# A transformer block on one core: gate/up with the activations held in TensorE, its product transposed by DMA

## The chip, the cores and the metric

The kernel runs on one core of one Trainium2 chip. The metric is the device time of one execution in microseconds; lower is better. Of the core's engines five appear below: TensorE (PE in the profile; PEld is its weight load), VectorE (DVE), ScalarE (ACT), GpSimd (POOL) and SyncE (SP), which here issues every DMA.

## The reference

One pre-norm block, sequence 2048, width 1024: attention with 32 query heads of 32 that share one key and value head, and a gated feed-forward of width 3584. All inputs and the output are bf16.

```python
def _A_ref(x, wq, wk, wv, wo):                 # H = 32, Dh = 32
    q = (x @ wq).reshape(B, S, H, Dh).transpose(0, 2, 1, 3)
    k = x @ wk
    v = x @ wv
    scores = jnp.einsum("bhqd,bkd->bhqk", q, k) * (Dh ** -0.5)
    p = _softmax(scores, axis=-1)
    o = jnp.einsum("bhqk,bkd->bhqd", p, v)
    return o.transpose(0, 2, 1, 3).reshape(B, S, H * Dh) @ wo
def _B_ref(x, w_gate, w_up, w_down):
    h = _sigmoid(x @ w_gate) * (x @ w_up)
    return h @ w_down
h  = x + _A_ref(_layernorm(x), A_wq, A_wk, A_wv, A_wo)
h2 = h + _B_ref(_layernorm(h), B_w_gate, B_w_up, B_w_down)
```

## The kernel before

**Tiles.** The sequence is cut into 16 query tiles of 128 tokens. Half a tile's heads (16) make a "half", so there are 32 halves; the two of one tile are a pair. For each half the loop runs over 16 key tiles. One such visit (`emit_S`, L650) is four matmuls of 512 columns, tiled four high in the array, into PSUM tile `S_ps`; two exponentials of 128x1024 on ScalarE (L668) write one of 12 buffers of `Pr` (a few other tiles serve as buffers at the start). `mk_PV` (L730) multiplies eight visits at a time with V, tiled four wide. Row sums of the softmax come in two ways: for halves in `RAW` (the first two) by matmuls with ones (the same `mk_PV`), for the others by adding the buffers on VectorE into `acc` (L643), then a selector matmul (`mk_SUM`, L694), a reciprocal, and a trip through DRAM that spreads the result (L707, L708). `mk_OP` (L818) is the output projection, to which the input is added; statistics and normalisation follow on VectorE and GpSimd (L337 to L356, L831), and a DMA transpose (L846) writes the normalised tile into `hnT`, with two tiles' room.

**Feed-forward.** The width 3584 is 7 groups of 512. `mk_GU` (L925) makes for each group a gate and an up group of matmuls: weights stationary (128x128), the tile's 128 tokens moving, so 32 matmuls of 128 columns into one PSUM bank of `F_ps`, whose output has the feed-forward channel on the partitions. ScalarE takes a tanh of the gate half (L961), VectorE multiplies (L967) and writes the product straight into `hact`, in the layout that the down projection reads. (A form with two tiles at once is in the code; the instructions of this kernel hold no matmul of that shape.) `mk_D` (L991) is the down projection: four groups of 28 matmuls of 256 columns, with `hact` stationary and the resident `w_down` (`wd_sb`) moving; VectorE adds the residual (L1004) and two DMAs store the tile (L1011).

**Weights.** Gate and up do not fit beside the rest and are loaded again for each tile, in slabs of 1 MB of four 256 KB loads each (`load_next`, L889, L908). Four slabs lie in `ring`; when the last visit has been issued, the buffers of `Pr` serve as slabs too. Tiles run the groups forth and back, so that two of seven are kept from one tile to the next.

**Order.** The program is written out by a planner (`Plan`) with costs of its own: each operation has an occupancy, a latency and a priority, and each engine's list is fixed when the program is built. A loop (L1044) gives TensorE one thing at a time: a visit when the planned backlog of ScalarE is under `run`, else the next matmul of the open group, else the next group of the queues `PV`, `SUM`, `OP`, `GU`, `D` and others. All groups but scores share the two banks of `F_ps`. Weight loads are paced in the plan (`pace`, bytes per ns), and the plan has a DMA rate (`rate`). SyncE's list is one queue in order: an issue that waits holds the ones behind it.

Of the kernel before, what the change touches and what calls it, by code (L numbers as in the profile page):

```python
# [12 lines left out]
P = 128  # L13
# [2 lines left out]
SEM = 75.0  # L16


TUNE = dict(swait=300, parts=2, raw=2, rl=0, nd=4, pc=16, rate=270, pace=280, xd=4, qf=2, dall=0, wo_late=1,
            nkn=3, few=0, rmin=700, hmin=1, h0=100, h1=350, hf=1.0, run=900, sum_few=0, pv_few=4, d_off=2,  # L20
            d_a=-1, d_b=0, eb=0, eq=700)


class Op:
# [16 lines left out]
class Plan:  # L41


    ENG = ("act", "dve", "pool", "sp")
    LATE = {"sl": 400.0, "rd": 300.0, "rb": 300.0, "hT": 400.0, "xt": 400.0}

    def __init__(self):
        self.lists = {e: [] for e in ("pe",) + self.ENG}
        self.free = {e: 0.0 for e in ("pe",) + self.ENG}
        self.heap = {e: [] for e in self.ENG}  # L50
        self.dma_free = 0.0
        self.pace_free = 0.0
        self.pe_mode = "dense"
        self.hold = (0.0, 0.0)
        self.seq = 0

    def op(self, eng, fn, deps=(), order=(), occ=60.0, lat=None, prio=5, key=None, nbytes=0, pace=False, tag=None):
# [23 lines left out]
    def need_end(self, d):  # L81
        while d.end is None:
            assert self.step(None), "plan is stuck"
        return d.end

    def start_of(self, o):

# [5 lines left out]
    def step(self, limit):  # L93
        best = None
        for e in self.ENG:
            h = self.heap[e]
            if h:
                s = min(self.start_of(o) for o in h)
                if best is None or s < best[0]:
                    best = (s, e)  # L100
        if best is None or (limit is not None and best[0] > limit):
            return False
        s, e = best
        h = self.heap[e]
        o = min((o for o in h if self.start_of(o) <= s + 1e-9), key=lambda o: (o.prio, o.seq))
        h.remove(o)
        if o.pace and self.pace_free > s:
            s2 = self.pace_free
            prev = [a for a in self.lists["act"][-6:] if a.end <= s2]
            if prev:  # L110
                o.deps.append(prev[-1])
            s = s2
        self.free[e] = s + o.occ
        o.start = s
        if o.nbytes:
            if o.pace:
                self.pace_free = s + o.nbytes / TUNE["pace"]
            go = max(s + 1500.0, self.dma_free)
            self.dma_free = go + o.nbytes / TUNE["rate"]
            o.end = self.dma_free + 750.0 + self.LATE.get(o.key.rstrip("0123456789"), 0.0)  # L120
        else:
            o.end = s + o.lat
        o.pos = len(self.lists[e])
        self.lists[e].append(o)
        for u in o.users:
            u.ready = max(u.ready, o.end)
            u.missing -= 1
            if u.missing == 0:
                self.heap[u.eng].append(u)
        o.users = []  # L130
        return True
# [21 lines left out]
def bass_sequential_preLN__grouped_kv_mqa__glu_gated_glu__prompt_kernel(  # L153
# [20 lines left out]
    NH = NT * 2  # L174
    NB = 3
    NHB = 3
    NSLAB = 4
    SW = 512
    NGR = NFT // 4
    NP = 12  # L180
    xf = A_x[0]
    of = out[0]

    with ExitStack() as es:
# [23 lines left out]
        hnT = SB("hnT", [DT, 2, P])  # L208
        hact = SB("hact", [NFT * 256])
        tnh = SB("tnh", [512], F32)  # L210
        st = SB("st", [8, 2, 6], F32)
        mv = SB("mv", [2, NT, 2], F32)
        mvb = SB("mvb", [2, NT, 2])
# [36 lines left out]
        pl = Plan()  # L250
        PE, ACT, DVE, POOL, SP = nc.tensor, nc.scalar, nc.vector, nc.gpsimd, nc.sync

        def dma(fn, key, nbytes, deps=(), prio=5, pace=False, order=()):
            return pl.op("sp", fn, deps, occ=450.0, key=key, nbytes=nbytes, prio=prio, pace=pace, order=order)

        def evac(fn_act, fn_dve, n, deps, prio, dve_rate=0.96, bias=0.0):
            now = pl.free["pe"]
# [126 lines left out]
        def x_by_dma(t):  # L384
# [2 lines left out]
                out=x_sb(t), in0=x_sb(t), scalar1=rstd[:, 0, t:t + 1], scalar2=None, op0=ALU.mult),  # L387
                [xcent[t], sv1[t][1]], prio=1, occ=330, lat=500)
            xT_ev[t] = dma(lambda: SP.dma_start_transpose(xnT[:, t // 4, :, (t % 4) * P:(t % 4 + 1) * P], x_sb(t)),
                           f"xt{t}", P * D * 2, [xnorm[t]], prio=0)  # L390
            ring_free(t)
            queue_after_xT(t)
            if t == NT - 1:
# [448 lines left out]
        def load_hT(t):  # L842

            if t not in hnorm or t in hT_ev or (t >= 2 and (t - 2) not in gu_last):
                return
            hT_ev[t] = hT_last[t] = dma(lambda: SP.dma_start_transpose(hnT[:, :, t % 2, :], hn[:, :]), f"hT{t % 2}", P * D * 2,  # L846
                                        [hnorm[t], gu_last.get(t - 2)] + (extra_rel if t < 2 else []), prio=0)


        ffn_next = [0]  # L850
# [3 lines left out]
        def start_ffn():  # L854
            t = ffn_next[0]
            if queues["GU"] or t >= NT or t not in hT_ev or (t and (t - 1) not in gu_last):
                return
            if t + 1 in hT_ev:
                ts = (t, t + 1)
            elif t + 1 in hnorm and hnorm[t + 1].end is not None:  # L860
                return
            else:
                ts = (t,)
            p = n_pass[0]
            n_pass[0] += 1
            ffn_next[0] += len(ts)
            load_next([])
            d_due.clear()
            nd = len(queues["D"])
            for i in range(NGR):  # L870
                for k in range(len(ts)):
                    mk_GU(p, ts, i, k)
            for k in range(nd):

                d_due.append(len(queues["GU"]) * (nd - k + TUNE["d_a"]) // (nd + 1 + TUNE["d_b"]))
# [3 lines left out]
        def group_of(p, i):  # L879
            return i if p % 2 == 0 else NGR - 1 - i  # L880
# [35 lines left out]
        hact_ev = {}  # L916
        box = {}

        def gu_deps(ts):
            return [d for t in ts for d in ([d_last[t - 2]] if t >= 2 else q_store[-NQS:] if t else extra_rel)]  # L920

        def gu_gate(p, ts, i, w):
            return (p, i, w) in slab_at and all((t == 0 or q_left[0] == 0) if t < 2 else d_done[t - 2] == ND for t in ts)

        def mk_GU(p, ts, i, k):  # L925

            gr = group_of(p, i)
            n = P * len(ts)
            fs = range(4) if len(ts) == 1 else range(2 * k, 2 * k + 2)
            f0 = 4 * gr + fs[0]  # L930
            hs = hact[:, :].rearrange("p (a f b) -> p a f b", a=2, b=P)[:, :, f0:f0 + len(fs), :]
            if len(ts) == 1:
                ho = hs[:, ts[0] % 2, :, :].rearrange("p f b -> p (f b)")
                mv_h = hnT[:, :, ts[0] % 2, :]
            else:
                ho = hs.rearrange("p a f b -> p a (f b)")
                mv_h = hnT[:, :, :, :]

            def shape(ap):
                return ap if len(ts) == 1 else ap.rearrange("p (a n) -> p a n", a=2)  # L940

            def bank_of(b, x):
                if len(ts) == 1:
                    return F_ps[:, b, x * P:(x + 1) * P]
                return F_ps[:, b, :].rearrange("p (a f b) -> p f a b", a=2, f=2)[:, x]

            def atoms(w):
                def a(b):
                    us, ops = slab_at[(p, i, w)]
                    return [(mm(bank_of(b, x), us[dt // 4][:, dt % 4, f * P:(f + 1) * P], mv_h[:, dt, :],  # L950
                                dt == 0, dt == DT - 1), n, "dense",
                             [ops[dt // 2]] if x == 0 and dt % 2 == 0 else [])
                            for x, f in enumerate(fs) for dt in range(DT)]
                return a

            def free(w, last):
                if i < NGR - 2 and fs[-1] == 3:
                    load_next([(u, [last]) for u in slab_at[(p, i, w)][0]])

            def after_g(b, last):  # L960
                box["a"] = pl.op("act", lambda: ACT.activation(out=tnh[:, :], in_=F_ps[:, b, :], func=ACTF.Tanh, scale=0.5),  # L961
# [2 lines left out]
                return [box["a"]]  # L964

            def after_u(b, last):
                e = pl.op("dve", lambda: DVE.scalar_tensor_tensor(  # L967
                    out=ho, in0=shape(tnh[:, :]), scalar=1.0, in1=shape(F_ps[:, b, :]),
                    op0=ALU.add, op1=ALU.mult), [last, box["a"]] + gu_deps(ts), prio=0, **t_dve(512))
                box["e"] = e  # L970
                for t in ts:
                    for f in fs:
                        hact_ev[(t, 4 * gr + f)] = e
                free(1, last)
                if i == NGR - 1 and fs[-1] == 3:
                    for t in ts:
                        gu_last[t] = last
                        load_hT(t + 2)
                        for dq in range(ND):
                            queues["D"].append(mk_D(p, t, dq))  # L980
                return [e]

            queues["GU"].append(Group("GU", atoms(0), lambda: [hT_ev[t] for t in ts] + slab_at[(p, i, 0)][1][0:TUNE["nkn"]], after_g,
                                      lambda: gu_gate(p, ts, i, 0)))
            queues["GU"].append(Group("GU", atoms(1), lambda: slab_at[(p, i, 1)][1][0:TUNE["nkn"]], after_u,
                                      lambda: gu_gate(p, ts, i, 1)))

        ND = TUNE["nd"]
        DW = D // ND
# [44 lines left out]
        def all_done(v):  # L1034

            v_done[0] = v
            if v == NV:
                all_S[0] = True
                load_next([(s.rearrange("p (d f) -> p d f", d=4), rel) for s, rel in free_slots])

        def known(deps, t):
# [208 lines left out]
```

## Time and profile before

| | |
|---|---|
| three runs | 1120.37, 1120.96, 1124.36 us (median 1120.96) |
| profiled execution | 1120.97 us, span 1118.9 us, TensorE clock 1.00 |
| TensorE busy | 1087.6 us (97%), 14987 instructions |
| TensorE weight load | 737.2 us (66%) |
| VectorE busy | 825.4 us (74%) |
| ScalarE busy | 1005.9 us (90%) |
| GpSimd busy | 57.8 us (5%) |
| DMA | 221.28 MB, mean 198 GB/s |

The span runs from the first to the last instruction; what lies around it is 2.07 us. A row of the page's groups reads: line, engine, operation, output<-input with shapes, count, then busy time and mean ns of one, then idle time ahead of it and what ended most of it. A matmul's mean is its passage through a pipeline, much longer than the spacing at which matmuls follow each other; spacing is read from the timeline, whose rows give a start, a length and a count. In a row of the busy time by stage, each engine has its busy us and number of instructions, then come the granted clock, the DMA engines' mean busy share and GB/s.

### The profile page before, as it was taken

What the parts mean: (1) busy time and instruction counts of PE and PEld (TensorE: products, weight loads), DVE (VectorE), ACT (ScalarE), POOL (GpSimd) and SP (SyncE); (2) the same over time, 40 slices, a digit from 0 to 9 for tenths busy, and PEclk for the clock granted to TensorE, in tenths of its full rate; (3) what the DMA queues carried; (4) which work ended last, traced back from release to release, by engine and by line L of the source; (5) the groups of instructions that cost most, each with busy time, mean ns of one, the idle gap of its engine ahead of it and who ended that gap; (6) DMA issues with size and microseconds to landing.
All of it is one profiled execution on the core that took longest, in us unless ns stands there. A gap on an engine that the chain in (4) does not pass through costs nothing.

```text
span 1118.9 us, 34515 instructions
## 1 busy us (share of the span) xinstructions
PE 1087.6 (97%) x14987; PEld 737.2 (66%) x15016; DVE 825.4 (74%) x1034; ACT 1005.9 (90%) x1155; POOL 57.8 (5%) x97
## 2 busy tenths in 40 slices
PE   6999998999999999999999999999999999999999
PEld 5533555756676766757666666766666766767898
DVE  8727888588878878688888778778788767877211
ACT  4898999999999999999999999999999999994010
POOL 5100100000000101010100001000001001000000
PEclk9999999999999999999999999999999999999999
DMA  9883695845848593846847495665747576479990
GB/s 257 184 272 114 149 309 180 258 144 181 265 122 253 161 282 88 254 136 206 234 124 218 128 282 140 212 207 163 209 140 218 154 219 201 142 219 288 289 291 16
DMA packets 244343, 221.28 MB, mean 198 GB/s; under 512 B 47456, under 2 KB 230752, under 8 KB 244192
## 3 DMA queue, kind: packets, MB, share of 16 engines
q1 hardware_dynamic: 244192, 219.07, 66.3%
q8 instruction: 119, 1.95, 0.7%
q14 instruction: 32, 0.26, 0.1%
HBM read 203.55 MB, written 8.11 MB: 189 GB/s over the span
## 4 chain that ended last, share of the span: by engine, by line
ACT 63%; PE 25%; DVE 5%; issue 5%; DMA 2%; SPq 1%; DVEq 0%
ACT Pr L668 59%; PE F_ps L416 22%; ACT tnh L961 4%; PE S_ps L416 3%; DMA rb<-r_scratch 1%; DVE acc L643 1%; DVE st L339 1%; DVE st L337 1%; SPq L708 0%; DVE ring L374 0%; DVE ring L386 0%; DMA ring<-in_B_w_gate_dram 0%; DMA ring<-in_A_x_dram 0%; PE F_ps L435 0%; DVE oun L759 0%
## 5 line engine op out<-in xcount | busy, mean ns | idle before, releaser
L668 ACT ACTIVATE Pr<-S_ps 128x1024 bf16<-128x1024 f32 x1008 | 957.7, 1193 | 6.3 <-PE S_ps L416 5.9
L643 DVE TENSOR_TENSOR acc<-acc,Pr 128x2048 bf16<-128x2048 bf16 x420 | 513.3, 1222 | 53.6 <-ACT Pr L668 39.6
L416 PE MATMUL F_ps<-hnT,ring 128*128 128x128 bf16 x6784 | 434.2, 219 | 2.1 <-issue 1.4
L416 PEld LDWEIGHTS F_ps<-hnT,ring 128*128 128x128 bf16 x6784 | 383.9, 98 | 67.0 <-issue 61.0
L416 PE MATMUL F_ps<-zone,hact 128*128 128x256 bf16 x1792 | 227.4, 273 | 0.1
L416 PE MATMUL S_ps<-QTb,kT 32*128 32x512 bf16 x2048 | 202.0, 385 | 7.1 <-ACT Pr L668 5.4
L416 PEld LDWEIGHTS F_ps<-zone,hact 128*128 128x128 bf16 x1792 | 162.8, 98 | 47.3 <-issue 27.8
L961 ACT ACTIVATE tnh<-F_ps 128x512 f32<-128x512 f32 x112 | 85.9, 767 | 75.2 <-PE F_ps L416 75.2
L967 DVE SCALAR_TENSOR_TENSOR hact<-tnh,F_ps 128x512 bf16<-128x512 f32 x112 | 76.5, 683 | 84.5 <-PE F_ps L416 83.4
L416 PE MATMUL F_ps<-Pr,Vt 128*32 128x512 bf16 x2016 | 133.4, 382 | 1.8 <-DVE h_sb L1004 1.0
L416 PEld LDWEIGHTS S_ps<-QTb,kT 32*128 32x128 bf16 x2048 | 51.5, 91 | 123.3 <-ACT Pr L668 86.7
L416 PEld LDWEIGHTS F_ps<-Pr,Vt 128*32 128x32 bf16 x2016 | 44.4, 96 | 57.0 <-issue 19.2
L416 PE MATMUL F_ps<-zone 128*128 128x512 bf16 (+3 forms) x572 | 73.7, 273 | 3.4 <-DVE mv L341 1.0
L416 PE MATMUL F_ps<-wo_sb,OT 128*128 128x512 bf16 x239 | 60.4, 380 | 3.8 <-DVE oun L759 1.4
L416 PEld LDWEIGHTS F_ps<-zone 128*128 128x128 bf16 x584 | 39.0, 98 | 30.3 <-issue 9.7
L350 POOL TENSOR_SCALAR zb<-mvb 128x1 bf16<-128x1 bf16 (+1 forms) x25 | 5.8, 233 | 986.8 <-DVE mvb L346 986.6
L1004 DVE SCALAR_TENSOR_TENSOR h_sb<-F_ps,h_sb 128x256 bf16<-128x256 f32 x64 | 26.9, 420 | 38.4 <-PE F_ps L416 38.2
L705 DVE RECIPROCAL r_sb<-F_ps 128x64 f32<-128x64 f32 x30 | 16.7, 558 | 36.2 <-PE F_ps L416 35.7
L416 PEld LDWEIGHTS F_ps<-wo_sb,OT 128*128 128x128 bf16 x256 | 21.6, 97 | 30.3 <-issue 8.1
L763 DVE TENSOR_TENSOR oun<-F_ps,oun 128x512 f32<-128x512 f32 x32 | 21.9, 686 | 21.8 <-PE F_ps L416 21.7
L643 DVE TENSOR_TENSOR acc<-Pr 128x2048 bf16<-128x2048 bf16 x30 | 35.0, 1165 | 0.0
L266 DVE CAST hact<-F_ps 128x512 bf16<-128x512 f32 (+1 forms) x25 | 16.3, 653 | 17.1 <-PE F_ps L416 15.2
(73 smaller groups left out, 329.9 us busy)
## 6 DMA issues: line engine op xcount, KB each, us to landing
ring<-in_B_w_gate_dram SPq DMA_DIRECT2D x304, 256.0 KB, 4.3
ring<-in_B_w_up_dram SPq DMA_DIRECT2D x304, 256.0 KB, 4.3
rb<-r_scratch SPq DMA_DIRECT2D x120, 64.0 KB, 2.7
zone<-in_B_w_down_dram SPq DMA_DIRECT2D x14, 512.0 KB, 4.8
Pr<-in_B_w_gate_dram SPq DMA_DIRECT2D x24, 256.0 KB, 4.6
Pr<-in_B_w_up_dram SPq DMA_DIRECT2D x24, 256.0 KB, 4.8
ring<-in_A_x_dram SPq DMA_DIRECT2D x16, 256.0 KB, 6.1
h_sb<-in_A_x_dram SPq DMA_DIRECT2D x16, 256.0 KB, 2.7
```

The costliest lines, as they stand in the source:

```text
L266: lambda: DVE.tensor_copy(out=out_ap, in_=in_ap))
L337: a = pl.op("dve", lambda s=s, src=src: DVE.bn_stats(st[:, s, 0, :], src[:, 0:512]), dp, prio=prio, occ=600, lat=756, order=[st_user.get(s)])
L339: b = pl.op("dve", lambda s=s, src=src: DVE.bn_stats(st[:, s, 1, :], src[:, 512:1024]), dp, prio=prio, occ=600, lat=756, order=[st_user.ge ...
L350: f = pl.op("pool", lambda: POOL.tensor_scalar(out=zb[:, ph, tk], in0=mvb[:, ph, tk, 1], scalar1=LN_EPS_BF16, scalar2=None, op0=ALU.add), ...
L416: return lambda: PE.matmul(o, lhsT=l, rhs=r, start=start, stop=stop, **kw)
L643: add_op[(hf, kt)] = pl.op("dve", lambda: DVE.tensor_tensor(out=a, in0=in0, in1=slot, op=ALU.add), dp, prio=6, **t_dve(2048, 1.92))
L668: exps[u] = pl.op("act", lambda i=i, pb=pb: ACT.activation(out=slot[:, i * 1024:(i + 1) * 1024].rearrange("p (a b) -> p a b", a=2), in_=S_ ...
L705: rc = pl.op("dve", lambda: DVE.reciprocal(r_sb[:, :], F_ps[:, b, 0:64]), [last, rd_ld.get(hf - 1)], prio=0, occ=64 * 8 / 0.96 + 20, lat=6 ...
L763: oun_ev[(hf, part)] = pl.op("dve", lambda: DVE.tensor_tensor(out=o, in0=F_ps[:, b, :], in1=o, op=ALU.add), [last, oun_ev[(hf, part - 1)]] ...
L961: box["a"] = pl.op("act", lambda: ACT.activation(out=tnh[:, :], in_=F_ps[:, b, :], func=ACTF.Tanh, scale=0.5), [last, box.get("e")], prio= ...
L967: e = pl.op("dve", lambda: DVE.scalar_tensor_tensor(out=ho, in0=shape(tnh[:, :]), scalar=1.0, in1=shape(F_ps[:, b, :]), op0=ALU.add, op1=A ...
L1004: e = pl.op("dve", lambda: DVE.scalar_tensor_tensor(out=h_sb[:, t % NHB, sl], in0=F_ps[:, b, 0:DW], scalar=0.5, in1=h_sb[:, t % NHB, sl], ...
```

## The change

Gate and up turn their operands around. The tile's normalised, transposed tokens (128x128 blocks of `hnT`) are stationary, and 512 columns of a weight slab move: 8 matmuls of 512 columns for a group in place of 32 of 128. The output then has tokens on the partitions. The product goes to one of three small buffers `act_s`, and a DMA transpose of 128x512 on SyncE's queue writes it into `hact` in the old layout; what waited for the product (the down projection) waits for that DMA. The form with two tiles is gone.

Beside this: the buffers of `Pr` are 11 instead of 12; `RAW` holds the first half only (`raw=1`), so the second half's sums go by VectorE adds and a selector matmul; transposes have a longer occupancy in the plan; near both ends (before 200 us of the plan, and after the last visit) the plan has another pace and rate than between; and several planner settings differ. The planner then writes all lists anew.

```diff
-TUNE = dict(swait=300, parts=2, raw=2, rl=0, nd=4, pc=16, rate=270, pace=280, xd=4, qf=2, dall=0, wo_late=1,
-            nkn=3, few=0, rmin=700, hmin=1, h0=100, h1=350, hf=1.0, run=900, sum_few=0, pv_few=4, d_off=2,
-            d_a=-1, d_b=0, eb=0, eq=700)
+TUNE = dict(pace0=280, rate0=300, swait=100, parts=2, raw=1, rl=0, nd=4, pc=16, rate=300, pace=250, xd=4, qf=2,
+            dall=1, wo_late=1, nkn=1, few=0, rmin=600, hmin=3, h0=200, h1=350, hf=1.0, run=700, sum_few=0,
+            pv_few=3, d_off=0, d_a=1, d_b=1, eb=0, eq=100)
...
+    def fast(self, s):
+
+        return s < 200000.0 or s > self.t_last
...
-                self.pace_free = s + o.nbytes / TUNE["pace"]
+                self.pace_free = s + o.nbytes / TUNE["pace0" if self.fast(s) else "pace"]
             go = max(s + 1500.0, self.dma_free)
-            self.dma_free = go + o.nbytes / TUNE["rate"]
+            self.dma_free = go + o.nbytes / TUNE["rate0" if self.fast(s) else "rate"]
...
+    NST = 3
...
-    NP = 12
+    NP = 11
...
+        act_s = SB("act_s", [NST, 512])
...
-                    us, ops = slab_at[(p, i, w)]
-                    return [(mm(bank_of(b, x), us[dt // 4][:, dt % 4, f * P:(f + 1) * P], mv_h[:, dt, :],
-                                dt == 0, dt == DT - 1), n, "dense",
-                             [ops[dt // 2]] if x == 0 and dt % 2 == 0 else [])
-                            for x, f in enumerate(fs) for dt in range(DT)]
+                    us, ops = slab_at[(t, i, w)]
+                    return [(mm(F_ps[:, b, :], hnT[:, dt, t % 2, :], us[dt // 4][:, dt % 4, :], dt == 0, dt == DT - 1),
+                             512, "dense", [ops[dt // 2]] if dt % 2 == 0 else []) for dt in range(DT)]
...
             def after_u(b, last):
+                k = n_act[0]
+                n_act[0] += 1
+                so = act_s[:, k % NST, :]
                 e = pl.op("dve", lambda: DVE.scalar_tensor_tensor(
-                    out=ho, in0=shape(tnh[:, :]), scalar=1.0, in1=shape(F_ps[:, b, :]),
-                    op0=ALU.add, op1=ALU.mult), [last, box["a"]] + gu_deps(ts), prio=0, **t_dve(512))
+                    out=so, in0=tnh[:, :], scalar=1.0, in1=F_ps[:, b, :],
+                    op0=ALU.add, op1=ALU.mult), [last, box["a"], act_dma.get(k - NST)], prio=0, **t_dve(512))
                 box["e"] = e
-                for t in ts:
-                    for f in fs:
-                        hact_ev[(t, 4 * gr + f)] = e
+                act_dma[k] = dma(lambda: SP.dma_start_transpose(ho, so), f"ha{t % 2}_{gr}", P * 1024, [e] + gu_deps(t),
+                                 prio=0, occ=700.0)
+                for f in range(4):
+                    hact_ev[(t, 4 * gr + f)] = act_dma[k]
...
             if v == NV:
                 all_S[0] = True
+                pl.t_last = pl.free["pe"]
```

## The prediction

> **What bounds the kernel now.** I read the page's slices and busy table first, then the chain that ended last, then the busy time by stage, then the timeline of TensorE.
>
> The slices (tenths busy, 40 slices of 28 us) and the groups that carry the work:
>
> ```profile
> PE   6999998999999999999999999999999999999999
> ACT  4898999999999999999999999999999999994010
> ACT 63%; PE 25%; DVE 5%; issue 5%; DMA 2%; SPq 1%; DVEq 0%
> L668 ACT ACTIVATE Pr<-S_ps 128x1024 bf16<-128x1024 f32 x1008 | 957.7, 1193 | 6.3 <-PE S_ps L416 5.9
> L416 PE MATMUL F_ps<-hnT,ring 128*128 128x128 bf16 x6784 | 434.2, 219 | 2.1 <-issue 1.4
> L416 PE MATMUL F_ps<-zone,hact 128*128 128x256 bf16 x1792 | 227.4, 273 | 0.1
> ```
>
> ScalarE is full until slice 36 (the exponentials), then nearly idle; TensorE is full to the end. The chain gives ScalarE 63% and TensorE 25%, the latter mostly at the end. So there are two stages: one in which exponentials and matmuls are both near their limit, and a tail that is TensorE alone. The stages, cut where score groups 1, 33, 97 and 481 start and where the last, the 512th, ends; the fourth row is a stretch of the tail:
>
> ```profile
> core 0: us, PE busy (x) PEld busy (x) DVE busy (x) ACT busy (x) POOL busy (x), PEclk, DMA share, GB/s
> 16.60:86.70 70.10, 66.94 (x718) 34.91 (x724) 40.56 (x104) 62.98 (x74) 11.41 (x18) 1.00 0.86 223
> 210.30:955.70 745.40, 737.36 (x10440) 498.49 (x10451) 587.63 (x675) 744.14 (x849) 29.97 (x36) 1.00 0.64 191
> 1016.50:1119.00 102.50, 98.72 (x1398) 90.78 (x1395) 31.23 (x49) 11.11 (x18) 1.34 (x3) 1.00 0.71 216
> 1020.00:1090.00 70.00, 69.05 (x1047) 63.60 (x1048) 23.15 (x36) 7.76 (x13) 1.34 (x3) 1.00 0.96 293
> ```
>
> Busy time cannot choose between the two engines in the middle: both are over 98%. The start-to-start spacing in TensorE's timeline can:
>
> ```profile
> 703.30 1.85 PE L416 MATMUL F_ps<-hnT,ring 128*128 128x128 bf16 x30
> 705.08 0.40 PE L416 MATMUL S_ps<-QTb,kT 32*128 32x512 bf16 x4
> 1097.15 3.22 PE L416 MATMUL F_ps<-zone,hact 128*128 128x256 bf16 x28
> 1100.21 3.74 PE L416 MATMUL F_ps<-hnT,ring 128*128 128x128 bf16 x64
> 1103.78 12.39 PE L416 MATMUL F_ps<-zone,hact 128*128 128x256 bf16 x112
> ```
>
> 64 gate/up matmuls from 1100.21 to 1103.78: 55.8 ns each. 28 down matmuls from 1097.15 to 1100.21: 109.3 ns each. 30 gate/up matmuls before a score group take 1.78 us, 0.11 more than 30 x 55.8 ns: that is what a change of tile position mode costs. In the same way a 512-column matmul (output projection) is 215.7 ns and a group of four tiled 512-column ones (scores, PV) 0.216. With these prices the counted work from 273 to 955 us fills all but 11.5 us. In the middle TensorE is packed, and ScalarE (64 exponentials x 0.905 plus 6.5 tanh x 0.48 = 61.0 us of a 62.1 us stretch per query tile) is just behind it.
>
> **The change, part by part.** I counted both programs' instruction orders with those prices, stage by stage. "Pair" is the two halves of a query tile (32 score groups).
>
> Gate/up: 7168 matmuls x 55.8 ns = 400.0 us become 1792 x 215.7 ns = 386.5: -13.5 us of TensorE. Weight loads fall to a quarter, but lay beside the matmuls already (PEld 67% of the middle), so nothing more for them. Row sums of the second half by ones-matmuls go to DVE adds and one selector sum: -64 tiled matmuls (16 groups x 0.216 = -3.5), +0.4. Total TensorE work counted: 1079.0 before, 1061.5 after.
>
> Where it goes (us; "counted" is TensorE's counted work):
>
> | stage | measured | counted | counted after | forecast |
> |---|---|---|---|---|
> | to first score | 16.6 | 4.4 | 5.6 | 17.8 |
> | pair 1 | 70.1 | 65.9 | 62.1 | 66.3 |
> | pair 2 | 62.3 | 60.7 | 60.1 | 61.7 |
> | pair 3 | 61.3 | 56.5 | 52.6 | 61.2 |
> | pairs 4-15 | 745.4 | 733.2 | 743.6 | 752.6 |
> | pair 16 | 60.8 | 59.9 | 60.3 | 61.2 |
> | last score to last matmul | 99.7 | 98.4 | 77.1 | 83.0 |
> | last store | 2.7 | - | - | 2.7 |
> | sum | 1118.9 | | | 1106.5 |
>
> To the first score: 7 more 256-column and 8 more 128-column matmuls stand ahead of it, +1.2. Pairs 1, 2 and 16 keep their stalls (4.2, 1.6, 0.9). Pair 3 is ScalarE's: 64 x 0.905 + 6 x 0.48 = 60.8 plus 0.4, so TensorE's saving of 4 there is lost. Pairs 4-15: the new order runs exactly one query tile of gate/up (112 matmuls) and down (112) in each pair, 61.95 us counted against 61.1; the stalls of 1.0 a pair shrink to 0.75, since those ahead of score and PV groups (3.3 of the 11.5 us) were waits on exponentials, and ScalarE (57.9 + 7 x 0.48 = 61.3) now has room. So the middle gets longer by 7 us: saved TensorE time is spent there on more feed-forward work. The tail gets it back: after the last score 960 gate/up matmuls (53.6) become 184 (39.7), 355 down (38.8) become 288 (31.5): -21.2.
>
> A second sum by ScalarE agrees: 4 more tanh (1.9) and 4 more evacuations (1.3) before the last exponential, first score 1.2 later: last score at 1016.5 + 4.4 = 1020.9; the table gives 1020.8.
>
> The tail's forecast is 77.1 + 1.4 (its old stalls) + 1.5 + 3. The 1.5 is new latency: the last product (0.68 us on DVE) now passes through a crossbar transpose before the down projection's last four matmuls of the first quarter can read it. Transposes of 256 KB land 3.1 to 5.7 us after issue, 128 KB stores in 2.4; I take 3.2 for 128 KB. Cover is 24 down matmuls, 2.6 us: 0.68 + 3.2 - 2.6 = 1.3, with a semaphore 1.5 (bounds 0.5 to 3.8). For earlier tiles and groups the transpose hides behind the next group (1.7 us) and behind down work that starts later.
>
> The 3 is DMA. The trace of before has 28 transposes, and one stands alone in a quiet stretch:
>
> ```profile
> 310.00:312.00 2.00, 2.00 (x35) 1.67 (x34) 0.54 (x2) 2.00 (x4) 0.00 (x0) 1.00 0.11 21
> 312.00:314.00 2.00, 2.00 (x36) 1.67 (x34) 0.00 (x0) 2.00 (x4) 0.00 (x0) 1.00 0.59 110
> ```
>
> 256 KB at share 0.59 + 0.11 over 2 us: 1.4 us of all engines; weight loads at 293 GB/s and share 0.96 cost 0.86 for 256 KB. So 0.7 us for each of the 112 new 128 KB transposes; a fit of share on bytes over all 2 us windows gives about 1.0 under load. The Trainium skill speaks otherwise (Advanced Engine Details and Errata, X-Bar Transpose (TRN2)): transposes run as fast as regular DMAs, 350-400 GB/s, an estimated 0.35 us each. By the page the new transposes take 39 us of DMA time in all, by the trace 78 to 112. In the middle neither matters: 7 transposes a pair add 5 to 7 us to DMA engines that are busy for 40 of 62 (share 0.64), and no wait for weights shows on TensorE. In the tail it does. After the last row sum 56 loads (48 us), 11 transposes, one of 256 KB (1.4) and five small rows (2): 56 us by the page, 59 to 63 by the trace. TensorE's work there is 72 us, of which the last 14 need no load, so 58 us. Before, 60 loads had 71 us by the same count and finished at about 1092, 10 us ahead of their last use. I take 3 us of stall (0 to 8).
>
> Costed at nothing: SyncE gets 112 issues x 0.65 us (half of the 1.3 us of a 256 KB one): 4.6 us of a 62 us pair in which loads take some 24. DVE gains 15 adds (1.2 us each) in pair 1, where it is 58% busy. One exponential buffer less: if that is not free it delays pair 1, where 2 us either way lie in the range. Other pacing of loads moves issues; TensorE showed no wait for them.
>
> Span 1106.5; the profiled execution took 1120.97 for a span of 1118.9, so 1108.6. That execution stands at the median (1120.96).
>
> **Rivals.** *Tail starved by DMA, or stalls in the middle that grow*: transposes cost 1.0 us or more under load, prefetch is thin (18 slabs left to use after the last sum, 14 of them still to load; before, 21 and 15), stall 8 instead of 3; or 1.2 us of stalls a pair instead of 0.75 (+5). For it: share 0.96 in the old tail. Against: the order holds down chunks between gate/up groups. 1113 to 1118.
>
> *Middle cheaper than counted*: stalls nearly vanish (0.3 a pair, -5), pair 1 falls to ScalarE's 62 (-4), tail without DMA stall (-3). 1097 to 1102.
>
> *Slower: SyncE's one queue.* Each transpose waits there for its DVE product, and the weight loads behind it wait too. In a dense gate/up stretch (699.8 to 709.2: 122 matmuls, 3.8 slabs) a slab is used up each 2.5 us, so the four-slab ring turns in 10; reissue takes 2.4 to 3.5 us and 4.3 to land, a margin of 2 to 3. Two transposes a round take 1.3 of it; if products come over half a microsecond later than their place, it is gone. It decides when the mean stall on TensorE passes 12.4 / 112 = 0.11 us a transpose; 0.2 gives 22 us, 1131. For it: order on SP is fixed. Against: SP sits waiting for buffer releases over 300 us in the waits, so it has time; no weight wait before.
>
> **How the numbers follow.** Forecast as summed (1103 to 1112): 0.58. Starved tail or middle stalls: 0.20. Cheaper: 0.13. SyncE queue: 0.09. 0.5% of 1121 is 5.6 us, about what a measurement here can tell from none. Faster by more (below 1115.4): 0.58 + 0.13 + two thirds of 0.20 = 0.84. Same: the rest of the 0.20 and a third of the 0.09, 0.10. Slower 0.06. The range leaves out a tenth on each side: 1100 to 1118.
>
> **What would show it.** Right: gate/up spacing 216 ns; last score at 1021 +-4; pairs 4-15 at 62.5 to 63; tail 80 to 86; a gap of 1 to 2 us on TensorE ahead of the last down matmuls. Wrong: TensorE waiting on weight DMA in the middle; score pairs above 64 us; a transpose landing after 5 us; tail over 90.

## The result, and the profile after

The changed kernel takes 1111.09 us (median of four runs, 1109.93 to 1111.60) against 1120.76 before: ratio 0.9905, 95% interval 0.9883 to 0.9927. The same kernel run again later (e5 below, called the control) gave 0.9901 (0.9887 to 0.9916). The forecast was 1108.6, range 1100 to 1118. The profiled execution took 1111.35 us with a span of 1109.6.

The page of the changed kernel, slices, chain and the three groups that answer to those shown before:

```profile
PE   5899987999999999999999999999999999999998
ACT  4899999999999999999999999999999999999110
PE 80%; ACT 9%; DVE 4%; DMA 4%; issue 2%; SPq 1%; POOL 0%; DVEq 0%; ACTq 0%
L675 ACT ACTIVATE Pr<-S_ps 128x1024 bf16<-128x1024 f32 x1008 | 945.6, 1061 | 9.3 <-PE S_ps L423 9.1
L423 PE MATMUL F_ps<-ring,hnT 128*128 128x512 bf16 x1672 | 413.6, 381 | 3.7 <-DMA ring<-in_B_w_gate_dram 2.5
L423 PE MATMUL F_ps<-zone,hact 128*128 128x256 bf16 x1792 | 231.0, 275 | 1.0 <-DMA hact<-act_s 0.6
```

The end of ScalarE's full stretch has moved one slice closer to the end of the span: the tail of TensorE alone is shorter. The chain has turned over, from ScalarE 63% and TensorE 25% to TensorE 80% and ScalarE 9%, although both engines are as busy as before. And new releasers stand behind the matmuls: weight DMAs (2.5 us) and the transposes (0.6 us).

Two pieces of TensorE's timeline (start, length, what, count):

```profile
309.14 2.12 PE L423 MATMUL F_ps<-ring,hnT 128*128 128x512 bf16 x9
311.19 0.40 PE L423 MATMUL S_ps<-QTb,kT 32*128 32x512 bf16 x4
...
1091.58 0.61 PE L423 MATMUL F_ps<-Pr,hnT 128*128 128x512 bf16 x2 [0.29 <-DMA Pr<-in_B_w_up_dram]
1092.47 1.32 PE L423 MATMUL F_ps<-Pr,hnT 128*128 128x512 bf16 x4 [0.29 <-DMA Pr<-in_B_w_up_dram]
1093.63 2.78 PE L423 MATMUL F_ps<-zone,hact 128*128 128x256 bf16 x24
1096.99 9.78 PE L423 MATMUL F_ps<-zone,hact 128*128 128x256 bf16 x88 [0.58 <-DMA hact<-act_s]
```

Nine gate/up matmuls and a mode change take 2.05 us: 9 x 215.7 ns + 0.11, the counted price. At the end two waits for weights (0.29 us each) and, after 24 down matmuls of the last tile, the wait for the last transpose: 0.58 us.

Busy time by stage: the third pair, pairs 4 to 15, and the last score to the end (busy us and instructions by engine, then clock, DMA share, GB/s):

```profile
150.20:215.90 65.70, 56.95 (x497) 21.82 (x496) 49.27 (x56) 62.25 (x71) 2.40 (x3) 0.95 0.91 236
215.90:964.50 748.60, 748.22 (x6722) 330.03 (x6721) 595.27 (x684) 747.86 (x853) 36.38 (x36) 1.00 0.80 211
1025.50:1109.60 84.10, 78.31 (x556) 48.14 (x552) 20.76 (x36) 8.73 (x14) 1.34 (x3) 1.00 0.90 240
```

The stages in us, where scores start and end as read from the timeline (the ends of the start and of the middle are exact to some tenths):

| | before | forecast | after |
|---|---|---|---|
| start: to the end of pair 3 | 210.3 | 207.0 | 215.9 |
| of it first score, pairs 1, 2, 3 | 16.6, 70.1, 62.3, 61.3 | 17.8, 66.3, 61.7, 61.2 | 19.5, 68.3, 62.4, 65.7 |
| middle: pairs 4 to 16 | 806.2 | 813.8 | 809.6 |
| tail: to the end of the span | 102.4 | 85.7 | 84.1 |
| span | 1118.9 | 1106.5 | 1109.6 |

The tail gives 18.3 us, the middle takes 3.4 back, the start 5.6. (The window of pairs 4 to 15 above ends 0.2 us short: pair 16 starts at 964.7.) Two questions follow: is the gain the cheaper matmuls, and what lengthens the start?

### The profile page after: what moved, and what is told of

It is laid out like the page before. It is cut to its first block, busy times and chain, and to the rows that moved or that the text cites. A ratio compares the mean times of both kernels' runs of the same rounds, so it can differ in the third digit from the quotient of the medians.

```text
span 1109.6 us, 23778 instructions
## 1 busy us (share of the span) xinstructions
PE 1076.8 (97%) x9608; PEld 488.4 (44%) x9608; DVE 836.5 (75%) x1039; ACT 1009.6 (91%) x1160; POOL 65.7 (6%) x97
## 4 chain that ended last, share of the span: by engine, by line
PE 80%; ACT 9%; DVE 4%; DMA 4%; issue 2%; SPq 1%; POOL 0%; DVEq 0%; ACTq 0%
PE F_ps L423 67%; PE S_ps L423 13%; ACT Pr L675 8%; DMA ring<-in_B_w_gate_dram 1%; DVE acc L650 1%; DMA rb<-r_scratch 1%; DVE st L344 1%; DVE st L346 1%; ACT tnh L944 1%; DMA Pr<-in_B_w_up_dram 0%; SPq L715 0%; DMA r_scratch<-r_sb 0%; SPq L907 0%; DMA ring<-in_A_x_dram 0%; DVE ring L381 0%
## 5 line engine op out<-in xcount | busy, mean ns | idle before, releaser
L675 ACT ACTIVATE Pr<-S_ps 128x1024 bf16<-128x1024 f32 x1008 | 945.6, 1061 | 9.3 <-PE S_ps L423 9.1
L650 DVE TENSOR_TENSOR acc<-acc,Pr 128x2048 bf16<-128x2048 bf16 x430 | 525.3, 1222 | 80.8 <-ACT Pr L675 65.8
L423 PE MATMUL F_ps<-ring,hnT 128*128 128x512 bf16 x1672 | 413.6, 381 | 3.7 <-DMA ring<-in_B_w_gate_dram 2.5
L423 PE MATMUL F_ps<-zone,hact 128*128 128x256 bf16 x1792 | 231.0, 275 | 1.0 <-DMA hact<-act_s 0.6
L423 PEld LDWEIGHTS F_ps<-ring,hnT 128*128 128x128 bf16 x1672 | 142.7, 98 | 192.6 <-issue 60.2
L423 PEld LDWEIGHTS F_ps<-zone,hact 128*128 128x128 bf16 x1792 | 163.9, 98 | 68.3 <-issue 34.2
L944 ACT ACTIVATE tnh<-F_ps 128x512 f32<-128x512 f32 x112 | 70.7, 631 | 57.3 <-PE F_ps L423 57.3
L953 DVE SCALAR_TENSOR_TENSOR act_s<-tnh,F_ps 128x512 bf16<-128x512 f32 x112 | 76.7, 684 | 39.5 <-PE F_ps L423 37.7
L423 PE MATMUL F_ps<-zone 128*128 128x512 bf16 (+3 forms) x584 | 76.4, 279 | 3.3 <-DVE Vt L273 1.9
L423 PE MATMUL F_ps<-wo_sb,OT 128*128 128x512 bf16 x256 | 63.8, 381 | 1.3 <-DVE h_sb L832 0.6
L729 DVE TENSOR_TENSOR OT<-oun,rb 128x512 bf16<-128x512 f32 x32 | 22.0, 689 | 18.3 <-DMA rb<-r_scratch 18.2
```

What stands on the lines that cost most here:

```text
L423: return lambda: PE.matmul(o, lhsT=l, rhs=r, start=start, stop=stop, **kw)
L650: add_op[(hf, kt)] = pl.op("dve", lambda: DVE.tensor_tensor(out=a, in0=in0, in1=slot, op=ALU.add), dp, prio=6, **t_dve(2048, 1.92))
L675: exps[u] = pl.op("act", lambda i=i, pb=pb: ACT.activation(out=slot[:, i * 1024:(i + 1) * 1024].rearrange("p (a b) -> p a b", a=2), in_=S_ ...
L729: ot_ev[hf] = pl.op("dve", lambda: DVE.tensor_tensor(out=OT[:, 4 * hh:4 * hh + 4, :], in0=o.rearrange("p (a b) -> p a b", a=4), in1=r.rear ...
L953: e = pl.op("dve", lambda: DVE.scalar_tensor_tensor(out=so, in0=tnh[:, :], scalar=1.0, in1=F_ps[:, b, :], op0=ALU.add, op1=ALU.mult), [las ...
```

## The experiments

Three sets of runs, each set on one chip and beside its own runs of the kernel before; "ratio" is to those, so versions of different sets are compared by their ratios. Stages are from one profiled execution of each, which lies up to 3 us from the median.

| | median us | ratio (95%) | start | middle | tail |
|---|---|---|---|---|---|
| before | 1120.8 | 1 | 210.3 | 806.2 | 102.4 |
| changed | 1111.1 | 0.9905 (0.9883-0.9927) | 215.9 | 809.6 | 84.1 |
| e1 turned, old settings | 1119.1 | 0.9957 (0.9942-0.9972) | 214.4 | 805.5 | 94.7 |
| e2 not turned, new settings | 1135.3 | 1.0103 (1.0086-1.0119) | 214.6 | 806.4 | 115.4 |
| e3 no transposes | 1107.3 | 0.9856 (0.9841-0.9871) | 215.1 | 808.8 | 82.3 |
| e4 copies for transposes | 1108.2 | 0.9864 (0.9849-0.9879) | 216.1 | 809.6 | 82.2 |
| e5 changed, control | 1111.6 | 0.9901 (0.9887-0.9916) | 216.2 | 809.9 | 84.3 |
| e6 dall=0 | 1109.2 | 0.9883 (0.9868-0.9899) | 213.4 | 809.9 | 83.6 |
| e7 raw=2 | 1123.9 | 1.0014 (1.0007-1.0022) | 219.0 | 812.2 | 90.2 |
| e8 replanned | 1113.5 | 0.9920 (0.9905-0.9936) | 215.8 | 809.1 | 85.5 |
| e9 cut in four | 1129.7 | 1.0073 (1.0056-1.0089) | 218.4 | 822.4 | 87.6 |
| e10 searched | 1110.1 | 0.9897 (0.9880-0.9914) | 213.5 | 810.2 | 84.6 |
| e11 turned, old settings, raw=1 | 1122.4 | 1.0008 (0.9999-1.0017) | 219.4 | 806.6 | 95.7 |
| e12 before, raw=1 | 1125.9 | 1.0040 (1.0024-1.0057) | 211.9 | 807.9 | 104.4 |

**Is the gain the turned operands? e1, e2 and e9.**

```diff
 e1, on the changed kernel
-TUNE = dict(pace0=280, rate0=300, swait=100, parts=2, raw=1, ... pace=250, ... dall=1, ... nkn=1, ... run=700, ...)
+TUNE = dict(pace0=280, rate0=270, swait=300, parts=2, raw=2, ... pace=280, ... dall=0, ... nkn=3, ... run=900, ...)
 e2, on the kernel before: the changed kernel's TUNE, NP = 11, its two-speed pacing and occupancy of transposes, and one tile at a time
-            if t + 1 in hT_ev:
+            if False:
                 ts = (t, t + 1)
```

> The changed kernel with its gate/up and transposes, but with the planner settings of before (rate and pace 270/280 throughout, raw=2, run=900 and so on; 11 exponential buffers). Theory (the turned operands pay, by less TensorE work): counted TensorE work 1065 us against 1079 before; counted tail 86.5; with the stalls of before the stages sum to a span of about 1108, so 1107 to 1113 us. Rival (the settings pay): the time stays at 1118 to 1124, as before, or more, if the old pacing starves the new matmuls. What also decides: where weights come late, TensorE waits on DMA in the third pair or the tail.

> The kernel before (gate/up weights stationary, 128 columns moving, one tile at a time, no transpose of the product) with the new planner settings, 11 buffers and the two-speed pacing. Theory (the turned operands pay): counted work 1076 us, and the tail is counted at 110 us (98 before), so slower than before: span about 1127, 1124 to 1132 us. Rival (the settings pay): 1108 to 1113.

The settings alone make it slower by 1.0% (e2), the turn alone faster by 0.4% (e1), both together faster by 1.0%. So the gain needs the turn, but the order has to be made for it. Both missed their theory's range. e2 lies 3 us above 1124 to 1132, with a tail of 115.4 us for 110 counted. e1 lies 6 above 1107 to 1113: pair 1 took 75.8 us, 5.7 more than before, and in its tail (94.7 us for 86.5 counted) TensorE waits for weights (total us, times, longest):

```profile
PE F_ps L423 <- DMA ring<-in_B_w_up_dram: 3.3, 2, 3.0
```

e2 shows the second thing: its start has first score 19.6, pairs 68.3, 61.8, 64.9, within 1 us of the changed kernel's. So the changed kernel's longer start came with the settings, without the turn or the transposes. (e1's start is longer too, 214.4, but in another place, pair 1.)

e9 takes the cheaper matmuls away and keeps order, DMA and layout:

```diff
-                    return [(mm(F_ps[:, b, :], hnT[:, dt, t % 2, :], us[dt // 4][:, dt % 4, :], dt == 0, dt == DT - 1),
+                    return [(mm4(F_ps[:, b, :], hnT[:, dt, t % 2, :], us[dt // 4][:, dt % 4, :], dt == 0, dt == DT - 1),
...
+        def mm4(o, l, r, start, stop):
+            def f():
+                for c in range(4):
+                    i = PE.matmul(o[:, c * P:(c + 1) * P], lhsT=l, rhs=r[:, c * P:(c + 1) * P],
+                                  start=start and c == 0, stop=stop and c == 3)
+                return i
+            return f
```

> The changed kernel in its own order, with each 512-column gate/up matmul cut into four of 128 columns with the same stationary block. Same arithmetic, same DMA, same layout; TensorE pays the fixed part of a matmul four times: 4 x 55.8 = 223 ns in place of 215.7, 13.5 us over 1792. Theory (TensorE bounds the middle and the tail, so the gain is the 13.5 us of fixed cost): a pair from 62.3 to 63.1 us, tail +1.4, 10 to 13 us more than the control, 1121 to 1124. Rival (ScalarE bounds the middle, at about 61.3 counted): pairs stay at 62.3 and only the tail shows it, 1112 to 1114.

It took 1129.7 us, 18 more than the control, which ran in another set; by the ratios it is 1.7%. 28 matmuls from 702.29 to 703.96 less a mode change are 55.8 ns each:

```profile
702.29 1.74 PE L428 MATMUL F_ps<-ring,hnT 128*128 128x128 bf16 x28
703.96 0.40 PE L423 MATMUL S_ps<-QTb,kT 32*128 32x512 bf16 x4
```

The 13 pairs of the middle grew by 12.5 to 12.8 us against the two profiles of the changed kernel; the count says 13 x 112 x 7.5 ns = 10.9. ScalarE's work is the same in both, so a middle that it bounds could not have grown: TensorE bounds it, and the gain is the fixed part that each matmul costs beside its columns: (4 x 55.8 - 215.7) / 3 = 2.5 ns. More came back than the 13.5 us counted, 3.5 in the tail (counted 1.4) and 2.4 at the start. In the tail TensorE waited 2.2 us for the last up weights, 0.6 in the changed kernel. At the start its clock stood at 0.50 in places where the changed kernel's did not (from 42 to 44 us, 0.50 against 1.00); what that costs was not tried.

**What do the transposes cost? e3 and e4.** Both keep the changed kernel's order and leave the product untransposed.

```diff
 e3, after the plan is made
+        lists["sp"] = [o for o in lists["sp"] if o.alt is None]          # alt: the multiply, set for each transpose
+                o.deps = [d.alt if d.alt is not None else d for d in o.deps]
 e4
-                act_dma[k] = dma(lambda: SP.dma_start_transpose(ho, so), f"ha{t % 2}_{gr}", P * 1024, [e] + gu_deps(t),
+                act_dma[k] = dma(lambda: SP.dma_start(ho, so.rearrange("p (f b) -> p f b", b=P)), f"ha{t % 2}_{gr}", P * 1024, [e] + gu_deps(t),
```

> The changed kernel's instruction order on every engine, with the 112 transposes of the product taken out of SyncE's list: the product is written to its place untransposed, and what waited for the transpose waits for VectorE's multiply. Theory (the stalls of the third pair and of the tail are DMA that the transposes fill up): 112 x 0.7 to 1.0 us of DMA time and 112 x 1.2 us of SyncE go; third pair 65.7 -> 62 us, tail 81 -> 79, 1105 to 1107 us against 1111. Rival (those stalls come from w_down and slab loads in themselves, and the transposes hide): third pair and time unchanged but for the 0.6 us wait ahead of the last down matmuls, 1110 to 1111.

> The changed kernel's order with each of the 112 transposes replaced by a plain copy of the same 128 KB between the same two tiles, in the same place of SyncE's queue (the product lies untransposed). Theory (a transpose costs more than a copy, on the queue and on the DMA engines): the copy issues in 0.4 to 0.6 us against 1.2 and takes about 0.45 us of DMA time against 0.7 to 1.0; most of what leaving it out gains comes back: 1106 to 1109 us. Rival (a transpose is as fast as a copy): same as the changed kernel within 1 us, 1110 to 1112.

Time against the changed kernel: 0.5% less without transposes, 0.4% less with copies. But not where e3's theory had it: the third pair stayed at 65.4 and 66.0. The gain is 2 us of tail in both. Before the tail e3 gained 1.7 to 2.3 us more, e4 0.5 at most; two profiles of the changed kernel differ by 0.6 there, and where e3 gains it was not tried. In the middle all three run at 62.2 to 62.3 us a pair. The prices, first of the changed kernel's transposes (128 KB, then the older 256 KB ones), then of e4's copies (issue on SyncE in ns and, for the 128 KB ones, time to landing in us, min/median/max), then DMA share and GB/s from 220 to 960 us in e3, e4 and the changed kernel:

```profile
L957 SPq DMA_TRANSPOSE hact<-act_s x112: 1189/1198/2631, 132.7 to 1094.5; - x112
DMA to landing us min/median/max: 2.4/3.8/6.2
L853 SPq DMA_TRANSPOSE hnT<-hn x16: 1238/1301/2392, 121.9 to 1051.0; - x16
L957 SPq DMA_DIRECT2D hact<-act_s x112: 465/471/1721, 133.1 to 1093.3; - x112
DMA to landing us min/median/max: 1.9/3.3/6.0
220.00:960.00 740.00, 728.81 (x6552) 326.47 (x6645) 593.27 (x680) 739.98 (x845) 36.52 (x36) 1.00 0.67 195
220.00:960.00 740.00, 728.01 (x6542) 325.79 (x6634) 591.89 (x680) 739.20 (x843) 36.52 (x36) 1.00 0.72 210
220.00:960.00 740.00, 739.62 (x6634) 325.78 (x6633) 590.27 (x679) 739.26 (x843) 36.38 (x36) 1.00 0.80 210
```

Some 83 products fall in these 740 us (7 in each 62.3). A copy of 128 KB takes (0.72 - 0.67) x 740 / 83 = 0.45 us of all DMA engines, a transpose (0.80 - 0.67) x 740 / 83 = 1.16 us, at equal bytes; the shares are rounded, so each is an estimate good to 0.1 us. (The lower matmul counts of the first two rows are records missing from those traces.)

**What lengthens the start? e5 and e6.** TensorE and the clock in the third pair of the changed kernel, and SyncE's last two loads of `w_down`:

```profile
186.07 0.42 PE L423 MATMUL F_ps<-acc,sel 128*32 128x64 bf16 x32
187.58 0.40 PE L423 MATMUL S_ps<-QTb,kT 32*128 32x512 bf16 x4 [1.09 <-ACT Pr L675]
189.42 0.40 PE L423 MATMUL S_ps<-QTb,kT 32*128 32x512 bf16 x4 [1.44 <-ACT Pr L675]
191.25 0.61 PE L423 MATMUL S_ps<-QTb,kT 32*128 32x512 bf16 x4 [1.44 <-ACT Pr L675]
192.32 3.14 PE L423 MATMUL F_ps<-zone,hact 128*128 128x256 bf16 x14 [0.46 <-issue]
195.39 0.61 PE L423 MATMUL S_ps<-QTb,kT 32*128 32x512 bf16 x4
...
183.89 2.20 SPq L516 DMA_DIRECT2D zone<-in_B_w_down_dram  x2
```

From 187 to 192 TensorE has nothing but scores: each waits 1.1 to 1.4 us for an exponential to free its PSUM bank. The first down matmul stands at 192.3. `w_down` is loaded in 512 KB pieces that take 5.0 us to land (median), the last of them issued in the row at 183.89, so all of `w_down` is there only at about 191 (an estimate): with `dall=1` the planner holds the first down projection until then, and puts it behind the score at 191.25. And then it is slow: 14 matmuls take 3.07 us to the next score, twice 14 x 109.3 ns. The rows by 2 us (PE and PEld first, granted clock third from the end) say why:

```profile
188.00:190.00 2.00, 0.40 (x4) 0.10 (x4) 1.79 (x3) 2.00 (x4) 0.00 (x0) 0.95 0.81 283
190.00:192.00 2.00, 0.61 (x4) 0.11 (x4) 1.23 (x1) 2.00 (x4) 0.00 (x0) 0.50 1.05 122
194.00:196.00 2.00, 2.00 (x12) 0.89 (x11) 1.20 (x1) 0.00 (x0) 0.00 (x0) 0.50 0.04 14
196.00:198.00 2.00, 2.00 (x19) 1.39 (x17) 0.00 (x0) 1.94 (x2) 0.00 (x0) 0.84 0.00 0
```

TensorE was busy 1.0 of 4 us, and its clock fell to 0.50. A mean of 0.95 over the row from 188 puts the fall at 189.8, and 0.84 over the row from 196 puts its end at 196.6: 6.8 us. Meanwhile ScalarE ran dry too (0.00 busy from 194 to 196), since no scores came. The Trainium skill (TensorE: Matmul & The Clock Gate, What's actually happening) describes such a gate, half rate after an idle window of about 3.4 us. The half rate agrees; the window here was not idle, since two score groups ran in the 3.3 us from 186.5 to 189.8. e6 takes the hold away:

```diff
-            dall=1, wo_late=1, nkn=1, ...
+            dall=0, wo_late=1, nkn=1, ...
```

> The changed kernel once more, as a control on the chip of the next three: 1110 to 1112 us if before takes 1121; spans by stage as in its first profile (first score 19.5, pairs 1 to 3 68.3, 62.4, 65.7, pairs 4 to 15 748.6).

> The changed kernel with one setting put back: dall=0, so the first down projection waits for the pieces of w_down as it reads them and not for all of them. Theory (the third pair is long because TensorE has nothing but scores to do while w_down lands, and its clock then halves): third pair 65.7 -> 62 to 63 us, granted clock 1.00 there, 3 us less in all, 1107 to 1109. Rival (the third pair is long because the slab loads and transposes fill the DMA engines, whoever waits): third pair stays over 65, time within 1 us of the control.

The third pair fell from the control's 66.2 to 63.4 us, just above the theory's 62 to 63 and under the rival's 65; in e10 below, which has `dall=0` too, it is 63.6. In e6 down matmuls stand between the same scores, at full speed (13 in 1.52 us to the next score), clock 1.00 (rows of e6: TensorE, then busy time from 190 to 196 us):

```profile
190.94 1.59 PE L423 MATMUL F_ps<-zone,hact 128*128 128x256 bf16 x13
192.46 0.40 PE L423 MATMUL S_ps<-QTb,kT 32*128 32x512 bf16 x4
...
190.00:196.00 6.00, 5.34 (x46) 3.48 (x47) 5.67 (x6) 6.00 (x8) 0.00 (x0) 1.00 0.14 44
```

The start is 2.8 us shorter, the middle is as before (809.9), and the time is 2.3 us less than the control's, the lowest median of the versions that leave no work out. Its interval overlaps the control's, so that this is the better kernel rests on the profile more than on the timing.

So `dall=1` accounts for 2 to 3 of the 4.5 us by which the third pair passed its forecast. About 2 are left in e6. They stand beside waits of TensorE for gate and up weights in that pair, first in the changed kernel, then in e6 (total us, times, longest):

```profile
PE F_ps L423 <- DMA ring<-in_B_w_gate_dram: 1.2, 2, 1.0
PE F_ps L423 <- DMA ring<-in_B_w_up_dram: 0.5, 1, 0.5
PE F_ps L423 <- DMA ring<-in_B_w_gate_dram: 1.2, 3, 0.8
PE F_ps L423 <- DMA ring<-in_B_w_up_dram: 0.8, 2, 0.5
```

The kernel before and e1 (turned, old settings) list no such wait in their whole start, and have third pairs of 61.3 and 61.8. That these waits make up the rest is read from the traces; no run takes them away alone.

**Single settings and new orders. e7, e8, e10, e11, e12.** Each diff is in the settings alone, but for e8, which also tells the planner a transpose's price.

```diff
 e7, on the changed kernel            -raw=1   +raw=2
 e11, on e1                           -raw=2   +raw=1
 e12, on the kernel before            -raw=2   +raw=1
 e8, on the changed kernel            -pace0=280, rate0=300, swait=100, pace=250, h0=200
                                      +pace0=300, rate0=315, swait=300, pace=270, h0=100
-                act_dma[k] = dma(..., P * 1024, [e] + gu_deps(t), prio=0, occ=700.0)
+                act_dma[k] = dma(..., P * 2048, [e] + gu_deps(t), prio=0, occ=1200.0)
 e10, on e6                           -rate=300, hmin=3, h0=200, pv_few=3, d_off=0, xd=4
                                      +rate=270, hmin=1, h0=300, pv_few=4, d_off=1, xd=6
```

> The changed kernel with one setting put back: raw=2, the second half's row sums by ones-matmuls again (64 tiled matmuls, 3.5 us, on TensorE in place of 15 adds on VectorE). Theory (adds are free there, TensorE is not, and with 11 buffers the buffers of the second half come back later): pair 1 from 68.3 to 72 to 76 us, the tail 3 us longer by count (80.6 against 77.1), 1117 to 1121 us in all. Rival (only the 3.5 us of TensorE count): 1113 to 1115.

> Turned operands and transposes with the planner settings of before, as in the first experiment, but raw=1. Theory (of the settings it is raw=1 that the turn needed, with 11 buffers): pair 1 from 75.8 to 71 or less, 4 to 6 us less than raw=2, 1113 to 1115. Rival (it is the order as a whole): within 2 us of raw=2, 1117 to 1121.

> The kernel before with raw=1 alone (12 buffers, old gate/up). Counted work 1075.8 us against 1079.0, the tail 100.1 against 98.4. Theory (raw=1 is worth something only where the order can use it): 1119 to 1124, no gain. Rival (a good part of the change's gain is raw=1): 1114 to 1117.

With the new settings raw=2 costs 12 us (e7), beyond what either theory gave: against the control 2.8 in the start (2.5 of it in pair 1), 2.3 in the middle, and a tail 5.9 longer where the count says 3.5. With the old settings it is raw=1 that costs, 0.5% by the ratios (e11 against e1), and the kernel before loses 0.4% by it (e12, 2 us above its theory's 1119 to 1124). So raw=1 alone isn't what the turn needs, and e11's theory fell; its rival had the kind right, but the time lies just above its 1117 to 1121. What raw is worth depends on the other settings, even in sign. Why raw=2 costs 12 us there stays open.

> The changed kernel with the planner told what a transpose costs here (1.2 us on SyncE's queue, DMA time of twice its bytes) and settings chosen anew for that (pace 270, 300 at the ends, rate 315 at the ends, swait=300, h0=100); nothing else differs. Counted: first score after 4.4 us of TensorE work as before the change, pairs 1 to 3 65.3, 58.6, 52.6, tail 77.1. Theory (the lost 8 us at the start belong to the order, not to the transposes): first score 16.6, pairs 69, 61, 63, middle and tail as the changed kernel, 1104 to 1107 us. Rival (the start is limited by DMA in any order): first score and pairs 1 to 3 sum to the same 216 us, 1110 to 1112.

> The changed kernel with dall=0 and planner settings searched around it (xd=6, rate=270, hmin=1, h0=300, pv_few=4, d_off=1). Counted: tail 74.5 us of TensorE work (77.1 in the changed kernel), middle the same 62.2 a pair, third pair 55.9. Theory (a tail shorter by count is shorter in time): tail 81 to 82 to the end of the span, third pair under 62, 1104 to 1108. Rival (weights come no faster, so a shorter tail only waits for them): tail as before, 1108 to 1110.

e8's theory fell, and the start came out as its rival had it: against the control, the first score came 2.4 us earlier, pair 1 took 3.7 longer, and the start summed to 215.8 for 216.2. (It kept `dall=1`, and its third pair was 65.2; the time lies 1.5 us above that rival's 1110 to 1112.) But the rival's reason, a start limited by DMA in any order, does not hold: e6 and e10 take 213.4 and 213.5. e10 had the shortest tail by count, 74.5, and took 84.6: TensorE waited 3.5 us for a transpose that was not back after 24 down matmuls, a wait the changed kernel has only at the very end. After it the clock was low, by the rows (1 - 0.56 + 1 - 0.59) x 2 / 0.5 = 3.4 us at 0.50. Here TensorE had run nothing for 3.5 us.

```profile
1056.92 1.04 PE L423 MATMUL F_ps<-zone,hact 128*128 128x256 bf16 x4 [3.50 <-DMA hact<-act_s]
1056.00:1058.00 2.00, 1.08 (x5) 0.74 (x6) 0.01 (x1) 0.00 (x0) 0.00 (x0) 0.56 0.97 276
1058.00:1060.00 2.00, 2.00 (x7) 0.72 (x6) 0.42 (x1) 0.00 (x0) 0.00 (x0) 0.59 0.94 307
1051.91 1.49 SPq L907 DMA_DIRECT2D Pr<-in_B_w_up_dram  x1
1053.44 1.20 SPq L957 DMA_TRANSPOSE hact<-act_s  x1
```

Its rival's time was right, but for another reason than the rival gave: the long wait was for the transpose, not for weights. VectorE had the product ready at 1051.5; the transpose was issued only at 1053.44, behind the issue of a weight load in SyncE's one queue.

## Why the prediction was right or wrong

It was 2.5 us too low, in range, and right on the mechanism of the gain. Its three stages were off by +8.9, -4.2 and -1.6 us; that the total came so close is in part luck, as these errors cancelled.

- *TensorE packed in the middle; fixed cost per matmul is the gain.* Right: 215.7 ns as counted, and e9 brought the cost back in the middle pair by pair. The prediction held that ScalarE was just behind; the chain of the changed kernel (PE 80%) and e9 say the same.
- *Middle longer, paid back in the tail.* Right in kind. Pairs 4 to 15 took 748.8 us, 3.8 under the 752.6: the term for stalls, 0.75 a pair, was too large. By the same count 5.2 us of stall were left in twelve pairs, 0.43 each; the waits ahead of the output projection went too (3.8 us before and 1.3 after, over the whole span), not only those for exponentials.
- *Tail.* 77.1 counted plus 5.9 forecast for stalls, latency and DMA; to the last matmul it took 81.2, so 4.1. By the spacing of matmuls the last transpose cost 0.7 for 1.5 forecast, the weights 0.9 for 3; two waits ahead of the output projection made 1.3.
- *Transposes hide in the middle, at any price the trace leaves open.* Right in time (62.2 to 62.3 us a pair in e3, e4 and the changed kernel), wrong in price. Issue was put at half of that of 256 KB, 0.65 us; it is 1.20, as good as independent of size. DMA time was put at 0.7 to 1.0 us; it is about 1.16, and the share rose to 0.80, not to 0.73 or 0.76. The page of the Trainium skill that the prediction set against the trace (Advanced Engine Details and Errata, X-Bar Transpose (TRN2): as fast as regular DMAs) does not hold for this shape: 1.16 us is 2 to 3 times the copy's 0.45. The prediction chose rightly to follow the trace, and even that was low.
- *"Pairs 1, 2 and 16 keep their stalls", "Pair 3 is ScalarE's".* This is the step that failed, 8.9 us in all. Pair 3 (+4.5) was to be bounded by ScalarE at 61.2. The forecast looked at how much work each engine had and not at when it could start: `dall=1` stands in the diff and was given no cost. It left TensorE dry, and then with half its clock; e6 shows 2 to 3 us of it. The other pacing of loads was put at nothing because TensorE showed no wait for weights before; in the start of the changed kernel it waits 3.0 us for them, 1.7 of it in pair 3 and 1.3 in pair 2 (+0.7). The first score (+1.7) and pair 1 (+2.0): what stands ahead of them was not followed one by one. In pair 1 TensorE's longest wait is 1.6 us for a part of V from VectorE (0.5 before). e2 and e8 place these with the settings and show that the two trade against each other; their single causes were not separated.
- *Rivals.* A tail starved by DMA: no, though e1's tail has it, 3.3 us. SyncE's queue: no, with nearly twice the issue time expected. A cheaper middle and tail: in part, 0.43 us of stall a pair and 0.9 us of weights in the tail; but pair 1 stayed at 68.3.

## What to carry to other kernels

When a stage is bounded by TensorE, count its instructions at start-to-start spacing, mode changes included: that gave the middle within 0.5% and the tail within 2 us, where busy shares (97% before and after) said nothing. Then, for each operation whose wait the change widens, write down when the last thing it waits for lands and what the engine has to do until then; here one setting that held the first down projection for all of its weights cost 2 to 3 us in a stage where the counted work had fallen. And give a planner the measured price of what it places, but expect no gain from it by itself (e8 had none): settings moved the time by up to 12 us, more than the change.

## What was not expected of the hardware

A crossbar transpose of 128 KB occupies its issuing queue for 1.20 us, one of 256 KB for 1.30; a copy of 128 KB takes 0.47. On the DMA engines it took about 1.16 us against 0.45 for a copy of the same bytes. TensorE's clock fell to 0.50 for 6.8 us in the midst of a kernel that keeps TensorE 97% busy, after 3.3 us in which it ran only two score groups; a wait of 3.5 us in e10 was followed by 3.4 us of the same.
